# Row 1's sums of the first norm on ScalarE, and four operation orders written anew

## The chip, the core and the metric

The kernel runs on one core of one Trainium2 chip. The metric is the time of one execution on the device in microseconds (us); times are medians over runs. The engines are PE (TensorE: PE for matmuls, PEld for weight loads), DVE (VectorE), ACT (ScalarE), POOL (GpSimd) and SP (SyncE, which here only issues DMAs). ACT and POOL issue DMAs too.

## The reference

Two pairs of layers on x, 2048 rows of 512 bf16 values:

```python
x = x + _A_ref(_layernorm(x), A_w_r, A_w_i)
x = x + _B_ref(_layernorm(x), B_w1, B_w2, B_w3, B_w4)
x = x + _A_ref(_layernorm(x), A_w_r, A_w_i)
x = x + _B_ref(_layernorm(x), B_w1, B_w2, B_w3, B_w4)
```

`_A_ref` is a two-dimensional real FFT over rows and columns, a product with complex weights, and the inverse FFT. `_B_ref` is an MLP mixer: norm, times w1 (512 by 512), gelu, a shift of the four quarters of the columns by -1, +1, -2, +2 rows, times w2, a residual sum; then norm, times w3 (512 by 1792), gelu, times w4, a residual sum.

## The kernel before

The 2048 rows lie as 128 partitions times 16 slots q ("rows" 0 to 15 below are these slots: 128 x 512 each). The FFT is done as matmuls with tables (T, FL, TL, TR, G, Tinv). The program is `first_front` (the norm and first transform of the input), then `layer` twice, called layer A (`last` false) and layer B (`last` true) here. A layer is one FFT mixing and one MLP mixing; layer A ends with the norm and first transform that layer B starts from.

No scheduler orders the work. Each stage is a small function with a letter, and the strings `ORDER_0`, `ORDER_A`, `ORDER_B` list them by hand-readable tokens: letter, number, for some the engine (A ScalarE, V VectorE, P GpSimd, D VectorE from PSUM), and after a dot the first PSUM bank. Each engine takes its own operations in the order of the string, and so does the DMA queue of SP; an operation that has to wait holds up all behind it on its engine.

Tokens of `ORDER_0`: `s` sums of a row (bn_stats on VectorE, L278, or for the rows in `ON_ACT` a mean and a square on ScalarE, L353 and L290), `i` their aggregation (L306), `f` the variance from ScalarE's sums of a group (three GpSimd operations, L359 to L361; after that of group 2 the first tables are loaded), `S` the square root on ScalarE (L365) and `J` the reciprocal on VectorE (L368) for a group of `GROUPS`, `Q` the scaled table Tq of a row (L384, L386), `O` the matmuls of a pair of rows (L403), `G` and `L` the copies from PSUM to V (two halves for the last ones). Behind them GpSimd issues the loads of `load_rest`: one doubling of W, a small copy that waits for the last Tq (L197), two operations that make half of TL (L238, L239, `turn_TL`), three more doublings (L185), a load of TL and the second load of TR (L184), which the `b` of units above 7 read.

Tokens of a layer, in the order of the data: `d` (L544 to L550), `t`, `q` (L568), `x`, `p` (product with W: L587 for V and P from a copy, L584 for D straight from PSUM), `b` and `V` (L598), `m` and `l`; `D` and `C` (L618), `Y`, `P` (L646), `a` (L654: x plus the transform, with row sums), `s` (L290); `r`, `e`, `i`, `M` the statistics of four rows, `n` the norm of a row (L374, L376), `T` the DMA transpose of two rows on SP (L674); `v` (w1, L686), `h` (gelu), `u` (w2, L702), `f` (L710), `k` (L290), `E` (L717), `R`, `o` (norm), `U` (transpose, L674), `w` (w3, L737), `g` (gelu, L744), `W` (w4, L757), `A` (L763), `y` (store). In layer A the next norm follows: `B` (L278), `j` (L306), `S`, `J`, `Q`, `O` (L413, L403), `G`, `L`, `I`. `N` makes the negative of a part of TR on VectorE (L817), `X` are matmuls on zeros. The `v` and `w` of a group of four rows need both transposes of that group.

Of the kernel before, what the change touches and what calls it, by code (L numbers as in the profile page):

```python
# [11 lines left out]
ACT = mybir.ActivationFunctionType  # L12
ALU = mybir.AluOpType
BF16 = dt.bfloat16
FP32 = dt.float32

P = 128
# [358 lines left out]
            self.K.nc.scalar.activation(dst, src, ACT.Identity, bias=self.mr[:, i, :], scale=r)  # L376


def scaled_T(K, q, r, eng="V"):

    K.Tq[q] = K.stream.tile([P, 2, P], BF16, name="Tq", bufs=8)
    if eng in "VP":
        e = K.nc.vector if eng == "V" else K.nc.gpsimd
        e.tensor_scalar(K.Tq[q][:], K.T[:], r, None, op0=ALU.mult)  # L384
    else:
        K.nc.scalar.activation(K.Tq[q][:], K.T[:], ACT.Copy, bias=0.0, scale=r)  # L386
# [65 lines left out]
def first_front(K):  # L452
# [71 lines left out]
def layer(K, last):  # L524
# [4 lines left out]
    V = K.V  # L529
# [6 lines left out]
    tv, X, pab, Y, xT, xT3, gT, ln, ln3, lnA = [{} for _ in range(10)]  # L536
# [251 lines left out]

    def scale_T(n, eng):
        k, i = divmod(n, 4) if n < 12 else (n, 0)  # L790
        scaled_T(K, ROWS[n], lnA[k].r[:, i:i + 1], eng)

    def front(k):
        qs = [ROWS[n] for n in PAIRS[k]]
# [24 lines left out]
    def act_table(k):  # L819
# [23 lines left out]
WAKE = 30  # L843
FILL = {}
GROUPS = [[0, 1], [2, 3], [4, 5, 6, 7], [8, 9, 10, 11], [12, 13], [14, 15]]
ON_ACT = [5, 9]
TABLES = 2
FIRST = [[0, 1], [2, 3], [4, 5], [6, 7], [8, 9], [10, 11], [12, 13], [14], [15]]
UNITS = {b: [b, b + 1] if 2 <= b < 14 else [b] for b in (0, 1, 2, 4, 6, 8, 10, 12, 14, 15)}
# [7 lines left out]
ROWS = [*range(2, 16), 0, 1]  # L857
PAIRS = {**{k: [2 * k, 2 * k + 1] for k in range(7)}, 14: [14], 15: [15]}
PLAIN = 6
FLEX = "mlGLnotxYIKEpQ"  # L860
FOLD = [(), ()]
ORDER_0 = """
s1 s0 i1 i0 S0 s2 s5 J0 Q0A Q1A s4 s7 s6 i4 f2 O0.4 i7 i6 S2 s3 J2 i2 s9 Q6V Q7V O3.0 i3 s11 S1 J1 s10 Q4A Q2A Q5A G3A
s8 i11 i10 i8 s12 f3 O2.2 Q3P O1.6 S3 J3 Q11P s13 i12 Q10A O5.0 s15 G0A i13 Q8A Q9P S4 G2A s14 i15 J4 Q12V i14 O4.4 S5
J5 Q15V G1A G5V Q13P O6.2 L5A O8.0 Q14V O7.6 G4A G6V G7A L7A G8V L6V L8V
"""
ORDER_A = """
d2.2 t2V d0.6 t0A d1.0 d4.4 N0 q0.6 t1A q2.2 d6.0 x0V p0V q1.6 t4A q4.4 x2A d10.2 t6A d8.0 p1D b1.6 p2P t10A b0.7
q10.2 p4D m0V t8A q6.0 d14.4 m1A d12.6 x10A t14V p10V x6A d15.2 t12A p6V b2.5 b4.3 m4A q14.0 q12.6 x14A q8.3 p12D b3.0
m2A b10.1 b11.5 x8A b7.4 t15A p14P q15.2 b5.6 b14.7 m10A b6.1 m11A b12.5 m7A m5A m3A b13.4 m6A p8V b8.6 m12A p15D b9.0  # L870
m8A b15.2 m15A V12.1 m13V V13.3 l12A m14V V15.4 V14.5 m9V l15V D3.0 l14V D1.6 l13A C1 C3 D0.2 C0 Y1A P3.4 P2.5 Y0A Y3V
a3 s3 P6.0 a2 s2 P1.1 P0.6 a1 a0 s1 P7.2 D2.4 C2 D5.6 s0 a7 s7 D7.2 C5 Y2V P5.1 r0 e0 i0 a6 Y5A a5 D4.4 s6 s5 P4.0 M0
n3V a4 n0V n2P s4 n1P D6.6 C7 C6 Y6A P11.0 T1 C4 P10.1 Y7V P15.2 r1 e1 a11 P12.3 i1 M1 n7V T0 Y4A n6V s11 n5A T3 P13.6
P9.5 n4V a10 s10 P8.4 a8 s8 v1.0 a9 s9 P14.7 a13 s13 h1 v0.4 a14 T2 c0 h0 r2 n8P v3.6 h3 v2.0 h2 n9V T4 a15 c1 n10V
n11V u0.5 a12 u3.4 u1.0 f3 u2.1 s12 f2 s14 s15 r3 n14V T5 v5.2 n15V v4.6 c3 T7 k3 h5 u4.1 n12V h4 u7.4 n13V f0 k0 T6
u6.5 f1 k1 u5.6 c2 E3V f7 E7V E2V f4 k2 R0 o2V f6 o3A v6.2 h6 v7.0 h7 f5 E1P E6V o1P k4 E0V o0V u12.4 k6 k7 k5 R1 U1
o7A u9.5 u15.3 f9 U0 u13.1 f12 E12V u10.7 k12 E4P u14.0 u11.5 o6P U3 E5V o5A f15 u8.2 w0.3 k15 E9P g0 f8 k8 o4P f11
E11V k11 w4.5 g4 w3.2 f14 k14 f10 w2.4 E10P g3 E8P w5.2 w1.6 g2 E14V g5 U2 w7.2 g1 f13 k13 R3 w6.0 k9 k10 w8.5 g6 W3.7
A3 B3 g8 W2.0 R2 A2 B2 o9P o10A W1.5 W0.0 g7 A1 B1 o11A U5 o8A j1 E15V U4 w14.2 g14 w11.4 w12.2 g11 w9.4 w10.6 g9 j2
w13.4 E13P g12 g10 g13 W7.1 o13V W5.2 A0 w17.4 W4.0 j3 B0 w16.6 j0 S0 Q2V Q3V A7 A4 Q1P B7 o12P W6.3 A5 A6 B6 g16 j7  # L880
w15.0 g15 w19.2 g19 B4 w18.0 g18 g17 w20.6 j4 j6 g20 o14A B5 W11.0 j5 S1 U6 Q6V W9.1 Q4P o15P U7 A11 B11 w21.6 Q5A
O2.2 O1.4 Q7A G1A j11 A9 B9 W8.0 G2A G2V Q0P O0.2 G1V A8 I1V I2V B8 j8 g21 w24.6 W10.1 A10 B10 j10 G0A g24 w23.6 j9 S2
Q11P Q9P g23 w22.0 O3.4 w26.6 g22 w27.0 G3A G3V G0V g26 Q8P I3V w25.4 g27 I0V g25 W13.2 A13 B13 j13 O4.0 G4A G4V I4V
W12.3 A12 B12 j12 S12 S13 J13 Q13P J12 W15.1 A15 B15 j15 S15 J15 Q15A W14.2 W24.5 Q12A Q10V O5.6 A14 A24 O6.2 G5A B14
B24 j14 S14 G6A J14 Q14A L6A O15.0 G15A L15A O14.2 G14A G5V I5V L14A
"""
# [17 lines left out]


# [28 lines left out]
```

## Time and profile before

| what | value |
|---|---|
| median of 3 runs | 345.87 us (345.47 to 346.12) |
| the profiled execution | 346.01 us, its span 344.2 us |
| granted TensorE clock, mean | 1.000 |
| first matmul of the first transform (L403) | 7.73 us |
| first matmul of layer A's products (L544) | 19.36 us, the next ones from 19.77 |
| first L618 of layer A | 37.06 us |
| first matmul of w1 in layer A (L686) | 51.76 us |
| first matmuls of layer B's products | 183.64 us |
| first matmul of w1 in layer B | 216.47 us |
| last operation of VectorE (L763) | 341.29 us, 0.29 us long |

Busy time in stretches, in us of each engine:

| stretch | PE | DVE | ACT | POOL |
|---|---|---|---|---|
| 0 to 10 | 7.59 | 5.65 | 4.96 | 3.54 |
| 10 to 20 | 9.68 | 8.69 | 8.96 | 7.93 |
| 20 to 30 | 10.00 | 9.07 | 8.96 | 7.19 |
| 30 to 40 | 10.00 | 8.53 | 8.59 | 1.92 |
| 185 to 200 | 14.47 | 13.98 | 14.93 | 5.50 |

Times in the profile count from the start of the span. Matmuls overlap in the records, so a busy PE can still hide small waits; the starts of the matmuls tell them. A few matmul records are missing, which shows as a gap of one pitch more.

### The profile page before, as it was taken

How to read it: one execution, taken by the hardware profiler on the slowest of the kernel's cores; microseconds unless marked ns; L12 is line 12 of the kernel's file. 1: busy time of each engine (PE TensorE's matmuls, PEld its weight loads, DVE VectorE, ACT ScalarE, POOL GpSimd, SP SyncE). 2: the span in 40 equal slices, each digit the busy share in tenths (PEclk: the TensorE clock that was granted, in tenths of full speed). 3: DMA queues.
4: the chain of work that ended last, by engine and by line, in shares of the span. 5: the costliest groups of instructions: out<-in, count | busy, mean ns of one | idle time of the engine just before them, and what ended most of it. 6: DMA issues, size and time to landing. Idle time of an engine off the chain costs nothing.

```text
span 344.2 us, 5699 instructions
## 1 busy us (share of the span) xinstructions
PE 335.5 (97%) x2171; PEld 187.6 (55%) x2189; DVE 165.0 (48%) x377; ACT 195.6 (57%) x357; POOL 107.1 (31%) x200
## 2 busy tenths in 40 slices
PE   7999999999999999999999999999999999999996
PEld 5878974444444444454467888444444444444443
DVE  4889895685035015264676979647802000110122
ACT  4979899768752403534538979968681446014300
POOL 2884066668242000304011404765591000000000
PEclk9999999999999999999999999999999999999999
DMA  7986986333030100300000002541403500000121
GB/s 257 314 295 230 372 202 113 72 61 62 3 61 0 32 0 0 31 2 0 2 0 2 2 3 47 104 81 20 89 0 76 109 0 0 30 18 5 41 78 46
DMA packets 45259, 24.60 MB, mean 71 GB/s; under 512 B 35072, under 2 KB 42240, under 8 KB 45232
## 3 DMA queue, kind: packets, MB, share of 16 engines
q1 hardware_dynamic: 43760, 19.74, 23.5%
q0 software_dynamic: 1232, 4.40, 3.7%
q8 instruction: 17, 0.28, 0.3%
q10 hardware_dynamic: 240, 0.10, 0.1%
q14 instruction: 10, 0.08, 0.1%
HBM read 11.61 MB, written 2.10 MB: 40 GB/s over the span
## 4 chain that ended last, share of the span: by engine, by line
PE 87%; DMA 4%; DVE 4%; ACT 2%; issue 1%; SPq 0%; POOL 0%; ACTq 0%; DVEq 0%; POOLq 0%
PE ps L737 28%; PE ps L757 26%; PE ps L686 8%; PE ps L702 8%; PE ps L598 4%; PE ps L403 3%; PE ps L618 3%; PE ps L568 2%; DMA xT<-xn 2%; PE ps L550 2%; PE ps L646 2%; DMA x_state<-in_A_x_dram 1%; DVE x_state L654 1%; ACT xn L290 1%; ACT gT L744 1%
## 5 line engine op out<-in xcount | busy, mean ns | idle before, releaser
L744 ACT ACTIVATE gT<-ps 128x1024 bf16<-128x1024 f32 x56 | 55.8, 1022 | 86.1 <-PE ps L737 86.1
L737 PE MATMUL ps<-xT,w 128*128 128x512 bf16 x448 | 99.2, 379 | 0.5 <-DMA xT<-xn 0.5
L757 PE MATMUL ps<-w,gT 128*128 128x512 bf16 (+2 forms) x462 | 97.8, 366 | 0.7
L763 DVE TENSOR_TENSOR x_state<-ps,x_state 128x512 bf16<-128x512 f32 (+2 forms) x34 | 22.2, 659 | 124.5 <-PE ps L757 124.5
L757 PEld LDWEIGHTS <-gT 128*128 128x128 bf16 x476 | 45.5, 98 | 51.4
L737 PEld LDWEIGHTS <-w 128*128 128x128 bf16 x448 | 43.7, 98 | 53.1 <-DMA xT<-xn 1.0
L710 DVE SCALAR_TENSOR_TENSOR xn<-xn,ln_c,ps 128x512 bf16<-128x512 bf16 x32 | 23.0, 743 | 15.5 <-PE ps L702 8.8
L686 PE MATMUL ps<-xT,w 128*128 128x512 bf16 x128 | 28.9, 379 | 0.7 <-DMA xT<-xn 0.4
L702 PE MATMUL ps<-w,hT 128*128 128x512 bf16 x124 | 28.3, 379 | 0.2
L290 ACT ACTIVATE junk<-xn 128x512 bf16<-128x512 bf16 x32 | 19.7, 622 | 4.8 <-DVE xn L710 4.8
L278 DVE BATCH_NORM_STATS2 ln_st<-x_state 128x6 f32<-128x512 bf16 (+2 forms) x31 | 20.2, 663 | 3.9 <-DMA x_state<-in_A_x_dram 3.6
L654 DVE SCALAR_TENSOR_TENSOR x_state<-ps,x_state 128x512 bf16<-128x512 f32 x32 | 20.7, 684 | 1.3 <-PE ps L646 1.2
L686 PEld LDWEIGHTS <-w 128*128 128x128 bf16 x128 | 12.3, 98 | 15.9 <-issue 1.7
L702 PEld LDWEIGHTS <-hT 128*128 128x128 bf16 x128 | 12.4, 98 | 15.3 <-ACT hT L693 0.4
L290 ACT ACTIVATE xn<-x_state 128x512 bf16<-128x512 bf16 x32 | 19.8, 620 | 0.9 <-DVE x_state L654 0.7
L693 ACT ACTIVATE hT<-ps 128x512 bf16<-128x512 f32 x32 | 17.4, 601 | 4.6 <-PE ps L686 4.4
L313 POOL TENSOR_SCALAR ln_ve<-ln_mv 128x4 f32<-128x4 f32 x11 | 2.8, 257 | 54.6 <-DVE ln_mv L306 53.9
L646 PE MATMUL ps<-Y,Tinv 128*128 128x256 bf16 x128 | 16.0, 272 | 0.1
L598 PE MATMUL ps<-TR,PB 128*128 128x128 bf16 x256 | 16.0, 219 | 0.0
L584 DVE TENSOR_TENSOR PB<-ps,W 128x1024 bf16<-128x1024 f32 x13 | 15.4, 1217 | 0.7 <-PE ps L568 0.5
L618 PE MATMUL ps<-G,hT 128*128 128x256 bf16 x128 | 15.7, 272 | 0.0
L403 PE MATMUL ps<-Tq,x_state 128*128 128x256 bf16 (+1 forms) x160 | 14.0, 246 | 1.6 <-ACT Tq L386 1.0
(95 smaller groups left out, 405.9 us busy)
## 6 DMA issues: line engine op xcount, KB each, us to landing
w<-in_B_w_dram SPq DMA_DIRECT2D x2, 1792.0 KB, 14.3
W<-W POOLq DMA_DIRECT2D x4, 514.0 KB, 5.0
x_state<-in_A_x_dram SPq DMA_DIRECT2D x8, 256.0 KB, 4.7
out_dram<-x_state SPq DMA_DIRECT2D x15, 128.0 KB, 1.9
w<-in_B_w_dram SPq DMA_DIRECT2D x2, 512.0 KB, 6.2
W<-in_A_w_r_dram SPq DMA_DIRECT2D x7, 128.5 KB, 5.8
W<-in_A_w_i_dram SPq DMA_DIRECT2D x7, 128.5 KB, 5.9
TL<-tab_TL POOLq DMA_DIRECT2D x3, 256.0 KB, 5.4
```

The costliest lines, as they stand in the source:

```text
L290: K.nc.scalar.activation(out, src, ACT.Square, bias=0.0, scale=D ** -0.5, accum_out=self.s[:, i, 1:2])
L403: K.nc.tensor.matmul(dst, lhsT=K.x[:, q, c * P:(c + 1) * P], rhs=rhs, start=(j == 0), stop=(j == 3))
L598: nc.tensor.matmul(o[:, k0 * P:(k0 + 1) * P], lhsT=pab[u][:, k, 2 * (b - u) + h, f * P:(f + 1) * P], rhs=K.TR[:, k:k + 2, 2 * b + h], star ...
L618: nc.tensor.matmul(o[:, i, e * 256:(e + 1) * 256], lhsT=M[:, F, e, 2 * m + i, :], rhs=K.G[:, F, e, :], start=(F == 0 and e == 0), stop=(F ...
L646: nc.tensor.matmul(o[:, h * 256:(h + 1) * 256], lhsT=K.Tinv[:, c], rhs=rhs[:, ::-1] if h else rhs, start=(e == 0), stop=(e == 1))
L654: nc.vector.scalar_tensor_tensor(K.x[:, q, :], ps.pop(("P", q)), 1.0, K.x[:, q, :], op0=ALU.mult, op1=ALU.add, accum_out=ln[g].s[:, i, 0:1])
L686: nc.tensor.matmul(o[:, i], lhsT=K.w1[:, t, j * P:(j + 1) * P], rhs=xT[g][:, :, t, :], start=(t == 0), stop=(t == 3))
L702: nc.tensor.matmul(o, lhsT=K.hT[:, j, st:st + P], rhs=K.w2[:, j, :], start=(j == 0), stop=(j == 3))
L710: nc.vector.scalar_tensor_tensor(xn[:, q, :], xn[:, q, :], ln[q // 4].c[:, q % 4:q % 4 + 1], ps.pop(("u", n)), op0=ALU.mult, op1=ALU.add, ...
L737: nc.tensor.matmul(o[:, i], lhsT=K.w3[:, c, t * P:(t + 1) * P], rhs=xT3[g][:, :, c, :], start=(c == 0), stop=(c == 3))
L744: nc.scalar.activation(gT[g][:, 2 * j:2 * j + 2, :], ps.pop(("w", k)), ACT.Gelu_apprx_tanh, bias=0.0, scale=1.0)
L757: nc.tensor.matmul(o, lhsT=gT[g][:, t, i * P:(i + 1) * P], rhs=K.w4[:, t, d], start=(t == 0), stop=(t == 13))
```

## The change

Row 1 joins `ON_ACT`, so that its sums are made by ScalarE instead of VectorE. `scaled_T` can make one half of the table alone (`signs=1`), and does so for the rows whose transform needs no more (rows n below 12 in layer A). All three orders are replaced; in them many operations change their engine and their place. The orders were made with a rule that an operation of VectorE and one of GpSimd that both work on SBUF exclude each other in time.

```diff
-def scaled_T(K, q, r, eng="V"):
+def scaled_T(K, q, r, eng="V", signs=2):
...
-    K.Tq[q] = K.stream.tile([P, 2, P], BF16, name="Tq", bufs=8)
+    K.Tq[q] = K.stream.tile([P, signs, P], BF16, name="Tq", bufs=8, padded_shape=[P, 2, P])
...
-        e.tensor_scalar(K.Tq[q][:], K.T[:], r, None, op0=ALU.mult)
+        e.tensor_scalar(K.Tq[q][:], K.T[:, 0:signs], r, None, op0=ALU.mult)
...
-        K.nc.scalar.activation(K.Tq[q][:], K.T[:], ACT.Copy, bias=0.0, scale=r)
+        K.nc.scalar.activation(K.Tq[q][:], K.T[:, 0:signs], ACT.Copy, bias=0.0, scale=r)
...
-        scaled_T(K, ROWS[n], lnA[k].r[:, i:i + 1], eng)
+        scaled_T(K, ROWS[n], lnA[k].r[:, i:i + 1], eng, 1 if n < 2 * PLAIN else 2)
...
-ON_ACT = [5, 9]
+ON_ACT = [1, 5, 9]
...
 ORDER_0 = """
-s1 s0 i1 i0 S0 s2 s5 J0 Q0A Q1A s4 s7 s6 i4 f2 O0.4 i7 i6 S2 s3 J2 i2 s9 Q6V Q7V O3.0 i3 s11 S1 J1 s10 Q4A Q2A Q5A G3A
-s8 i11 i10 i8 s12 f3 O2.2 Q3P O1.6 S3 J3 Q11P s13 i12 Q10A O5.0 s15 G0A i13 Q8A Q9P S4 G2A s14 i15 J4 Q12V i14 O4.4 S5
-J5 Q15V G1A G5V Q13P O6.2 L5A O8.0 Q14V O7.6 G4A G6V G7A L7A G8V L6V L8V
+s0 s1 i0 s5 s2 s3 s4 i3 i2 f0 S0 S1 i4 J0 Q0A Q1A s7 J1 Q3A O0.5 Q2A O1.0 s6 i7 i6 f2 S2 s9 f3 s10 J2 i10 Q5A Q4V O2.2
+s11 s8 Q6V G0A i11 i8 S3 s13 Q7A J3 Q8A G1A i13 O3.4 s12 i12 S4 s14 Q9P O4.6 s15 i14 Q10A G3A i15 S5 J4 Q12V J5 Q11P
+Q13V O5.0 G2A L5V O6.4 Q14P O7.2 G4A G7A G5V Q15V L7A O8.0 G8A G6V L6V L8A
 ORDER_A = """
-d2.2 t2V d0.6 t0A d1.0 d4.4 N0 q0.6 t1A q2.2 d6.0 x0V p0V q1.6 t4A q4.4 x2A d10.2 t6A d8.0 p1D b1.6 p2P t10A b0.7
...
-m2A b10.1 b11.5 x8A b7.4 t15A p14P q15.2 b5.6 b14.7 m10A b6.1 m11A b12.5 m7A m5A m3A b13.4 m6A p8V b8.6 m12A p15D b9.0
...
-P9.5 n4V a10 s10 P8.4 a8 s8 v1.0 a9 s9 P14.7 a13 s13 h1 v0.4 a14 T2 c0 h0 r2 n8P v3.6 h3 v2.0 h2 n9V T4 a15 c1 n10V
...
-w15.0 g15 w19.2 g19 B4 w18.0 g18 g17 w20.6 j4 j6 g20 o14A B5 W11.0 j5 S1 U6 Q6V W9.1 Q4P o15P U7 A11 B11 w21.6 Q5A
...
-W12.3 A12 B12 j12 S12 S13 J13 Q13P J12 W15.1 A15 B15 j15 S15 J15 Q15A W14.2 W24.5 Q12A Q10V O5.6 A14 A24 O6.2 G5A B14
-B24 j14 S14 G6A J14 Q14A L6A O15.0 G15A L15A O14.2 G14A G5V I5V L14A
+d2.3 d0.6 d1.2 N0 t2V d4.0 t0A q0.6 t1V q2.4 d6.2 t4A x2A q1.0 p0D t6A d10.6 t10A q4.4 d8.2 t8A p1D d12.0 q10.6 p4D
...
+p6V p12D b11.5 b10.1 b7.0 x8A m10A q15.6 m5A x15A b6.2 p8V b12.1 m12A b3.4 m6V p15V m11A b9.3 b13.1 b8.2 b14.5 m7V m3A
...
+a5 s5 C4 n1P r1 T0 D7.2 n2V P10.1 n3V C7 P11.0 Y4V Y7A D6.6 C6 P9.2 e1 P8.4 i1 M1 P15.3 a11 a9 Y6A n4P P13.7 T1 n5A
+P12.0 T2 a10 a8 a13 s11 n6P s9 s8 n7P s10 P14.5 r2 a14 n9V v1.1 h1 v0.5 a15 T3 h0 s13 v3.1 c0 n11V s15 h3 v2.4 n10V T5
...
+o10A g2 w11.0 g11 w7.2 g7 g5 w10.0 w12.2 g12 W1.7 A1 B1 j1 o8A U4 E12V w13.4 g13 o12P U7 W0.6 A0 B0 W2.2 w9.5 g9 W3.3
+o11P U5 E13V o13A U6 A2 B2 A3 j0 B3 j2 j3 S0 Q0V Q3V w8.4 w20.6 g10 Q1V g8 w14.0 w19.2 g20 w15.4 g14 W5.0 A5 W7.6 g19
...
+W14.0 G4V I4P A12 B12 j12 S12 J12 A13 W24.4 Q12A B13 J15 Q15A Q10V j13 S13 J13 A14 A24 B14 O5.2 B24 j14 G5A O15.6 G15A
+L15V Q13P O6.0 S14 J14 Q14A O14.4 G6A L6A G5V G14A L14A I0P I5V
 ORDER_B = """
-X3.4 d4.1 d15.0 t15V d12.5 d1.7 t4A q4.0 t1V t12A q15.2 d0.4 d2.6 p15D x4A q1.0 d8.2 t0A q0.4 t2A t8A q2.6 p1D x0A
-q12.0 x12A d10.2 q8.4 p2D d14.0 p4P b4.1 d6.6 p12V m4V t10A x8A b3.2 b5.5 q10.3 t6A t14A q6.6 m5A b12.0 m3A b2.1 m12A
-b1.5 p8V b8.0 p0P b9.2 x6A b0.6 b15.7 m8A p10D q14.3 m1A p6V m9A p14D b11.0 m2A b10.2 m0A b6.1 b7.6 b14.3 m11A m10V
...
+X6.6 d15.2 d1.1 d4.4 t15A q15.6 p15D d12.2 t1A d0.0 t4A q4.4 t0V t12A q1.6 x4A p1D d2.1 t2A d14.0 t14A d8.4 q0.6 x0A
+q12.2 x12A q2.0 p4V b5.6 m5A b15.7 m15A t8V q8.4 x8A d10.6 t10A d6.2 p0P b1.4 p2D t6A b4.1 b0.0 m0A p8V q10.6 p12V
+q6.2 b2.0 m1A m4A x6A b8.4 p10D b3.1 b12.5 b9.3 b13.2 p6V q14.6 m2A b11.0 m12A m11V b10.5 m3A m8A x14A b7.1 p14V m9A
...
+P15.2 n1P a11 s11 P14.7 T2 a8 v2.3 a10 a15 s8 T1 s10 c0 r2 T0 v3.5 a12 s15 v1.1 n11P n10V s12 h2 T5 c1 a13 h1 v0.3 h3
...
```

No instruction is added beside the three operations of GpSimd and the two of ScalarE for row 1's sums (in place of VectorE's), and three matmuls on zeros; the rest moves between engines and places.

## The prediction

> **What bounds the kernel now.** I read the page first, its busy shares and slices, then the table of stretches, then TensorE's waits, then the chain that ended last.
>
> ```profile
> PE 335.5 (97%) x2171; PEld 187.6 (55%) x2189; DVE 165.0 (48%) x377; ACT 195.6 (57%) x357; POOL 107.1 (31%) x200
> ...
> PE   7999999999999999999999999999999999999996
> PEld 5878974444444444454467888444444444444443
> DVE  4889895685035015264676979647802000110122
> ACT  4979899768752403534538979968681446014300
> ```
>
> TensorE is busy 97% of the span; VectorE and ScalarE come near full in two places, slices 2 to 6 and 22 to 25 (8.6 us each): the first norm with the Fourier products of layer A, and the Fourier products of layer B. Everywhere else they idle beside TensorE. No matmul is added or taken but three fillers (X3.4 becomes X6.6, 3 x 0.11 us, in a wait). So the change is worth what it does to TensorE's waits, and I counted these from the starts of the matmuls (each start minus the start before, less the usual pitch): 0.07 us from 60 to 85, nothing from 85 to 140 and from 240 to the end, 1.4 from 140 to 185, 3.1 from 185 to 200, about 1 each in 40 to 60 and 200 to 240. TensorE begins real work at 7.73. The new orders can gain or lose only there, and a new wait in a quiet stretch counts in full.
>
> ```profile
> PE ps L403 <- ACT Tq L386: 1.0, 2, 0.8
> ...
> PE ps L403 <- DVE Tq L384: 0.6, 1, 0.6
> PE ps L568 <- DVE PB L584: 0.5, 1, 0.5
> PE ps L737 <- DMA xT<-xn: 0.5, 1, 0.5
> PE ps L686 <- DMA xT<-xn: 0.4, 1, 0.4
> ```
>
> These are the longest waits: in us, how often, the longest. Each is a place to follow in the new orders. I did so by hand: every engine takes its operations in the written order, each with the duration of its row before.
>
> **The first norm (the named part).** Before, row 1 is a bn_stats on VectorE (0.66). After, it is two activations on ScalarE (L353, L290), 1.23 a row as row 5 shows (5.96 to 7.19), and three small GpSimd operations (L359 to L361), ending about 0.75 after the sums (f2: 7.19 to 7.95). Rows 0 and 1 land at 4.2, so row 1's sums run 4.22 to 5.45, row 5's (landed 5.9) 5.92 to 7.15; S0 was at 5.76 and now stands behind them: 7.15 to 7.44. S1 goes in front of Q0A, J0 behind s2, s3, s4, i3, i2, i4 on VectorE: J0 7.54, Q0A 7.74 to 8.23. First matmul 8.28 against 7.73: **0.55 later**. But Q3A (8.53) and Q2A (8.93 to 9.42) follow at once, so O1 starts with no wait at O0's end, 9.6; before, TensorE stood still until here:
>
> ```profile
> 9.78 9.12 PE ps L403 x108
> 18.92 0.72 ACT V L154 x2
> ```
>
> From there I find each Tq ready in time (0.1 lost at row 7), O8 ends at 18.8, L6V and L8A end at 19.35, and layer A's products start at 19.45 instead of 19.77: **-0.3**.
>
> **What hangs on the last Tq.** GpSimd's loads wait for it (gate, L197): Q14V ends at 17.57 before, Q15V at 18.05 after. Then come turn_TL (1.63 and 0.75), three W doublings, TL2 and the second TR load, which is just in time now:
>
> ```profile
> TR<-tab_TR POOLq DMA_DIRECT2D x1, 768.0 KB, 7.9
> ```
>
> Issued at 23.26, landed 31.1; its first user, b10, starts at 31.21. GpSimd waits 0.72 before the last doubling, which takes up part of a delay; from below nothing, from above 0.5 plus a 0.5 meeting with N0: it lands at 31.1 to 32.1. The products themselves, followed unit by unit, bring b11 to 31.45 (gaps at d10, q14 and b5) and the next stage, D1, to 37.05, where D3 starts at 37.06 before: the 0.3 is gone there. With TR 0 to 0.6 late I take **+0.2** at this point (bounds 0 and 0.6).
>
> N0, a VectorE operation from SBUF to SBUF, now stands before t2V and meets turn_TL; in the trace it runs at 21.71, after turn_TL's end at 20.2, so no row shows that meeting. The Trainium skill ("SBUF — State Buffer", section "Who interferes with whom") says that GpSimd and such an operation hold a shared port in turn and the second waits for the whole instruction. By it N0 waits until 19.98, the loads move 0.5 more, and the forecast would be 345.4. A nearer row for a meeting is n3V beside n1P at 46.08: 0.83 instead of 0.41, 0.42 lost; the loads' bound above is that row, rounded up.
>
> **The first MLP's entry.** All sixteen P now stand before v1; before, P14 stood after it while v1 waited 0.56 at 51.76 for T0. T1 lands at 51.75 after (n2V, n3V end at 47.75, two transposes of 1.26 and 3.3 to landing). h1 no longer stands behind s13, v3 waits for T3 (55.4) about 0.1. The first u comes at 59.0 instead of 59.27: **-0.3** (bounds -0.5 and 0).
>
> **The last transpose of layer A.**
>
> ```profile
> 138.79 2.86 ACT gT L744 x3
> 141.65 0.70 ACT xn L376
> ...
> 142.42 4.57 DMA xT<-xn
> ...
> 147.03 1.90 PE ps L737 x8
> ```
>
> Row 15's norm (o14A) stood behind three gelus, its transpose landed at 147.0, and w21 waited: the start gap there is 0.67 over pitch. After, U7 is written before W0 and U6 after B0, some 20 us ahead of w27, their first user: **-0.65**. Unless another wait takes its place (nothing I followed does), all of it is gained.
>
> **From layer A to B.** After the last W4, A24, B24, j14, S14 stay; L15V (0.42) is put before J14, and G6A and L6A behind Q14A, where G15A and L15A stood (0.5 each against 0.27). L14A ends at 183.65 against 183.86, but I5V ends at 183.75 against 183.50. d15 starts around 183.5 to 183.8 against 183.64: **-0.1** (bounds -0.3 and +0.3).
>
> **Layer B's products.** Here the exclusion is to be seen:
>
> ```profile
> 192.13 2.20 DVE L587 TENSOR_TENSOR PB<-X,W 128x2048 bf16<-128x2048 bf16 x1
> ...
> 194.85 1.21 DVE L587 TENSOR_TENSOR PB<-X,W 128x2048 bf16<-128x2048 bf16 x1
> ```
>
> ```profile
> 187.74 5.50 POOL L587 TENSOR_TENSOR PB<-X,W 128x2048 bf16<-128x2048 bf16 x2 [10.54 <-ACT X L154]
> ```
>
> The same VectorE product takes 2.20 while GpSimd's p0P runs (to 193.24) and 1.21 alone: 0.98 lost, in a chain of VectorE operations without a gap (p2D, p12V, m4V, p8V, p10D) at whose end TensorE waits 0.69 at 198.38. After, p4 goes from GpSimd to VectorE (1.22), t8 too (1.22 against 0.69 for t15), p14 reads SBUF (0.69 against 1.21), and copies go to ScalarE and back; p0P runs beside t8V and p2D, which read PSUM. VectorE's sum is 17.4 against 17.1 with the 0.98 in it; ScalarE's grows by 0.2. So the loss is not simply gained: it is spent on p4. Following the units I get D3 at 201.3 against the first D at 202.17, **-0.9**; by the sums alone it is +0.15. I take half, -0.45, as I cannot rule out small gaps of 0.1 on a chain of 30 operations.
>
> **Layer B's MLP entry.** v2 waits for its transpose at 216.47; followed through a4 to a7, r1, e1, i1, n7P, n6P, T3, T2, it starts at 216.4: 0 (bounds -0.3, +0.3). The first w3 (244.5 before, U1 landed 244.03) has U1 at 243.5 and w6 at 244.1 after: no wait. Norms on GpSimd go from 3 to 5 in A and 3 to 6 in B; each meeting with VectorE costs 0.42 by the row above, off the path where I followed it. Rows 0, 1 and the last W4s, the A20 and its store are as before: tail 0.
>
> **Sum.** Front to D1 +0.2, MLP entry -0.3, w21 -0.65, hinge -0.1, B's products -0.45: -1.3. Waits that I did not find can only add; I put 0.2 for them: **-1.1**. Against the profiled execution's own 346.01 (span 344.2 and 1.8 around it) this is **344.9**; the median before is 345.87, 0.14 lower, so about -0.3%. A change under 0.2% (0.7 us) cannot be told from none.
>
> **Rivals.**
> 1. *The walk holds in full* (nothing lost to small gaps, B's products -0.9, TR in time): 0 - 0.3 - 0.65 - 0.1 - 0.9 = -1.95, 344.1. For it: TensorE's slack everywhere else; against: both vector engines 90% full there. Chance 0.17.
> 2. *No change*: B's products +0.15 because VectorE's sum did not shrink, TR 0.6 late, the rest as forecast: 0.6 - 0.3 - 0.65 - 0.1 + 0.15 + 0.2 = -0.1, 345.9. Chance 0.26.
> 3. *The first norm comes late and takes the loads along* (slower). S0 waits for ScalarE's four sums, S1 stands before Q0A, J0 behind four bn_stats: every Tq depends on one in-order chain. If the last Tq comes 2 us later than my 18.05, d2 starts 1.7 after 19.77, turn_TL, the doublings and TR come 2 late, and b11 waits as long: +2.2 in place of +0.2 gives 346.9. From about 1.1 us late it outweighs the gains, from 1.65 the result is slower by over 0.2%. For it: J0 and S0 move by over 1.2 us; against: rows 2 to 5 are summed by then, and TensorE has O0's 1.3 us to cover. Chance 0.22.
> The forecast itself: 0.35. That the exclusion is already absent in other places or not the planner's doing changes nothing here; the written orders are what runs.
>
> So faster 0.17 + 0.35 = 0.52, within 0.2% 0.26, slower 0.22. The range runs from rival 1 with the MLP entry at its bound of -0.5 (343.9) to rival 3's 346.9.
>
> **What would show it.** First matmul of L403 near 8.3 and hardly a gap after it; first L544 near 19.4; no wait at the first b over 7 (L598 near 31.4); no 0.5 us wait for a transpose in L737; no VectorE L587 over 1.3 us; the first L618 of layer B under 18 us after its first L544. I am wrong if a wait appears between 85 and 140 or after 240, where there is none now, or if L598 waits for TR.

## The result, and the profile after

Six runs of the changed kernel have a median of 343.89 us (343.40 to 344.89), six of the kernel before 346.32 (345.47 to 347.24). The ratio is 0.9945, with a 95% interval of 0.993 to 0.996: about 1.9 us faster by the ratio (1.4 to 2.4 by its interval; the two medians lie 2.4 apart). The profiled execution took 344.65 us with a span of 342.9, against the forecast 344.9, and the granted clock was 0.999. Another set of runs of the same program, with its own runs of the kernel before (345.87), gave 344.52 and 0.9957 (0.994 to 0.9974); its profile has a span of 341.9. The page of the changed kernel:

```profile
PE 334.4 (98%) x2175; PEld 187.0 (55%) x2192; DVE 163.2 (48%) x370; ACT 195.8 (57%) x360; POOL 108.2 (32%) x210
...
PE   6999998999999999999999999999999999999996
...
DVE  5889794577005212544387989665812000010122
ACT  6979899687651521522438989978771343146000
```

The busy shares hardly moved: VectorE has 1.8 us less, GpSimd 1.1 more. They tell nothing of the gain. TensorE's waits do:

```profile
PE ps L403 <- DMA x_state<-in_A_x_dram: 1.8, 1, 1.8
PE ps L686 <- DMA xT<-xn: 1.0, 1, 1.0
PE ps L262 <- DVE zeros L253: 1.0, 1, 1.0
PE ps L598 <- DMA TR<-tab_TR: 0.4, 1, 0.4
```

The waits for Tq inside the first transform, for PB at L568 and for xT at L737 are gone. In their place stand one wait ahead of the first transform, one of 1.0 at the first w1 (L686) of layer A, and 0.4 for TR. (The one on the zeros comes before any real work.) The start gaps over pitch, summed by stretch, say where it matters (the sums depend a little on which pitch is taken as the usual one): 0.7 to 0.8 us less than before from 185 to 200 and 0.8 to 1.0 less from 140 to 185, but 0.6 to 0.8 more from 20 to 40 and some 0.4 more from 40 to 60; nothing from 60 to 140 and from 240 on, so no new wait in the quiet stretches.

The following table sets the predicted terms beside the profiles. A term is the difference to before in the time between two checkpoints (first matmuls of a line; D1 is the first L618 of A):

| stretch | predicted | after | the same program again |
|---|---|---|---|
| start to D1 (before 37.06) | +0.2 | +0.10 | -0.04 |
| D1 to the first w2, L702, of A (22.05) | -0.3 | +0.35 | -0.56 |
| from there to layer B's first L544 (124.53) | -0.75 | -0.99 | -0.99 |
| layer B's products, to its first L618 (18.37) | -0.45 | -0.50 | -0.50 |
| from there to its first L686 (14.47) | 0 | -0.20 | -0.20 |
| from there to the last matmul (124.56) | 0 | -0.12 | -0.06 |
| not found | +0.2 | | |
| sum | -1.1 | -1.35 | -2.33 |

Only the second line differs much between the two profiles of the same program. That is the wait of 1.0 at L686.

### The profile page after: what moved, and what is told of

Read it like the earlier page. It is cut to its first block, busy times and chain, and to the rows that moved or that the text cites. A ratio compares the mean times of both kernels' runs of the same rounds, so it can differ in the third digit from the quotient of the medians.

```text
span 342.9 us, 5718 instructions
## 1 busy us (share of the span) xinstructions
PE 334.4 (98%) x2175; PEld 187.0 (55%) x2192; DVE 163.2 (48%) x370; ACT 195.8 (57%) x360; POOL 108.2 (32%) x210
## 4 chain that ended last, share of the span: by engine, by line
PE 86%; DMA 8%; ACT 2%; SPq 2%; DVE 1%; issue 1%; POOL 0%; POOLq 0%; DVEq 0%
PE ps L737 28%; PE ps L757 28%; PE ps L686 8%; PE ps L702 8%; PE ps L598 4%; DMA W<-in_A_w_i_dram 3%; PE ps L618 3%; DMA TR<-tab_TR 2%; PE ps L646 2%; PE ps L568 1%; ACT xn L290 1%; PE ps L550 1%; DMA T<-tab_T 1%; DMA xT<-xn 1%; SPq L231 1%
## 5 line engine op out<-in xcount | busy, mean ns | idle before, releaser
L737 PE MATMUL ps<-xT,w 128*128 128x512 bf16 x448 | 99.0, 379 | 0.0
L737 PEld LDWEIGHTS <-w 128*128 128x128 bf16 x448 | 43.8, 98 | 52.9
L686 PE MATMUL ps<-xT,w 128*128 128x512 bf16 x128 | 28.7, 379 | 1.0 <-DMA xT<-xn 1.0
L702 PE MATMUL ps<-w,hT 128*128 128x512 bf16 x124 | 28.2, 379 | 0.2
L686 PEld LDWEIGHTS <-w 128*128 128x128 bf16 x128 | 12.3, 98 | 16.2 <-issue 1.7
L278 DVE BATCH_NORM_STATS2 ln_st<-x_state 128x6 f32<-128x512 bf16 (+2 forms) x30 | 19.4, 663 | 3.7 <-DMA x_state<-in_A_x_dram 3.3
L702 PEld LDWEIGHTS <-hT 128*128 128x128 bf16 x128 | 12.4, 98 | 15.2 <-ACT hT L693 0.5
L598 PE MATMUL ps<-TR,PB 128*128 128x128 bf16 x256 | 16.0, 219 | 0.4 <-DMA TR<-tab_TR 0.4
L618 PE MATMUL ps<-G,hT 128*128 128x256 bf16 x128 | 15.9, 272 | 0.0
L598 PEld LDWEIGHTS <-PB 128*128 128x128 bf16 x256 | 14.5, 98 | 2.2 <-issue 2.0
```

The lines of the kernel that those rows point to most:

```text
L598: nc.tensor.matmul(o[:, k0 * P:(k0 + 1) * P], lhsT=pab[u][:, k, 2 * (b - u) + h, f * P:(f + 1) * P], rhs=K.TR[:, k:k + 2, 2 * b + h], star ...
L618: nc.tensor.matmul(o[:, i, e * 256:(e + 1) * 256], lhsT=M[:, F, e, 2 * m + i, :], rhs=K.G[:, F, e, :], start=(F == 0 and e == 0), stop=(F ...
L686: nc.tensor.matmul(o[:, i], lhsT=K.w1[:, t, j * P:(j + 1) * P], rhs=xT[g][:, :, t, :], start=(t == 0), stop=(t == 3))
L702: nc.tensor.matmul(o, lhsT=K.hT[:, j, st:st + P], rhs=K.w2[:, j, :], start=(j == 0), stop=(j == 3))
L737: nc.tensor.matmul(o[:, i], lhsT=K.w3[:, c, t * P:(t + 1) * P], rhs=xT3[g][:, :, c, :], start=(c == 0), stop=(c == 3))
```

## The experiments

Two theories were to be told apart. Mine: the gain is made of one-place repairs (a transpose asked for earlier, a VectorE product kept clear of a GpSimd one), and the part that the change is named for carries nothing. The rival: the front carries the gain, through everything that hangs on the last Tq. All ratios are to the kernel before, run on the same chip, with 95% intervals. In the diffs, three dots stand for lines left out, and of some lines of an order only the tokens that matter are shown.

**The three parts, each alone.** The kernel before with the new front, row 1 on ScalarE and the new `ORDER_0`:

```diff
-ON_ACT = [5, 9]
+ON_ACT = [1, 5, 9]
...
 ORDER_0 = """
-s1 s0 i1 i0 S0 s2 s5 J0 Q0A Q1A s4 s7 s6 i4 f2 O0.4 i7 i6 S2 s3 J2 i2 s9 Q6V Q7V O3.0 i3 s11 S1 J1 s10 Q4A Q2A Q5A G3A
...
+s0 s1 i0 s5 s2 s3 s4 i3 i2 f0 S0 S1 i4 J0 Q0A Q1A s7 J1 Q3A O0.5 Q2A O1.0 s6 i7 i6 f2 S2 s9 f3 s10 J2 i10 Q5A Q4V O2.2
...
```

> The kernel before with the new ORDER_0 and row 1 in ON_ACT alone; layers A and B keep their old orders. Theory (the front's gain is taken back by the second TR load, which waits for the last Tq and for the loads of W): the first L544 comes 0.5 to 0.6 us earlier than 19.36, the first b above 7 waits for TR (31.7 against 31.21), the first L618 is at 37.1 to 37.6 as before or later, and the time is unchanged to 0.5 us longer (ratio 1.000 to 1.0015). Rival (the named part carries the gain): the 0.5 to 0.6 us reach the first L618 and the end, ratio 0.998.

Measured: 0.9994 (0.998 to 1.0007). The path of the theory is not in this profile: rows 4 and 5 landed late, the first L544 came at 19.59 and not half a microsecond earlier, and no wait for TR is in the list. The first L618 is at 37.22, as expected.

The kernel before with layer A's new order and the half tables:

```diff
-def scaled_T(K, q, r, eng="V"):
+def scaled_T(K, q, r, eng="V", signs=2):
...
 ORDER_A = """
-d2.2 t2V d0.6 t0A d1.0 d4.4 N0 q0.6 t1A q2.2 d6.0 x0V p0V q1.6 t4A q4.4 x2A d10.2 t6A d8.0 p1D b1.6 p2P t10A b0.7
...
+d2.3 d0.6 d1.2 N0 t2V d4.0 t0A q0.6 t1V q2.4 d6.2 t4A x2A q1.0 p0D t6A d10.6 t10A q4.4 d8.2 t8A p1D d12.0 q10.6 p4D
...
```

> The kernel before with the new ORDER_A and the halved Tq alone. Theory (parts add up, and A's gain is the wait of w21 and the hinge to layer B, less a later first u): first u up to 0.4 us later than 59.10, no wait in L737, the first L544 of layer B 0.4 to 0.9 us earlier than 183.64, ratio 0.9975 to 0.999. The transpose T0 took 2.16 us to issue in the profile after, against 1.23 to 1.33 for all others: if that is due to the order it is 2.1 to 2.2 here again, and v1 waits over 1 us; if it was chance, it is 1.3 and v1 starts near 51.8. Rival (the gain comes with the front or layer B): ratio 1.000 or above.

Measured: 0.9968 (0.9956 to 0.998), a larger gain than expected. L737 has no wait, and from the first w2 to layer B it takes 123.80 us against 124.53. In the profile this is lost again, as the first w2 is 0.8 late and the first L544 of layer B at 183.69: T0 took 2.33 us, which the expectation would have read as the order's doing; but the next kernel, with layer A's old order, has 2.14, so the order is not the cause.

The kernel before with layer B's new order:

```diff
 ORDER_B = """
-X3.4 d4.1 d15.0 t15V d12.5 d1.7 t4A q4.0 t1V t12A q15.2 d0.4 d2.6 p15D x4A q1.0 d8.2 t0A q0.4 t2A t8A q2.6 p1D x0A
...
+X6.6 d15.2 d1.1 d4.4 t15A q15.6 p15D d12.2 t1A d0.0 t4A q4.4 t0V t12A q1.6 x4A p1D d2.1 t2A d14.0 t14A d8.4 q0.6 x0A
...
```

> The kernel before with the new ORDER_B alone. Theory (the product that stood still beside GpSimd's is freed, and the entry of the MLP is a little earlier): L587 on VectorE nowhere over 1.3 us, from the first L544 of layer B to its first L618 17.8 to 18.0 us instead of 18.36, end 0.7 to 0.9 us earlier, ratio 0.9975 to 0.998. Rival (what was taken from the exclusion was put back on VectorE as p4, nothing gained): 18.3 to 18.5 us, ratio 0.9995 to 1.0005.

Measured: 0.9977 (0.996 to 0.9993), as expected; layer B's products took 17.72 us, and no L587 of VectorE in them took over 1.3 (one in layer A's products, at 28.4, took 1.61). The three gains, 0.0006, 0.0032 and 0.0023, add to 0.006, and the whole change has 0.0055: within their intervals the parts add. The named one shows no gain of its own; its interval allows at most 0.002.

**Why the front earns nothing.** In the changed kernel ScalarE and TensorE begin so:

```profile
5.63 0.63 ACT L353 ACTIVATE junk<-x_state 128x512 bf16<-128x512 bf16 x1
...
6.88 0.54 ACT L365 ACTIVATE ln_r<-ln_mv,eps 128x2 f32<-128x2 f32 x2
7.39 1.71 ACT L386 ACTIVATE Tq<-T,ln_r 128x256 bf16<-128x256 bf16 x4
```

```profile
7.95 1.26 PE L403 MATMUL ps<-Tq,x_state 128*128 128x256 bf16 x13 [1.76 <-DMA x_state<-in_A_x_dram]
```

The columns are start, duration, engine, line, operation; the bracket is the idle time before it and what ended it. Row 5's sums start the moment rows 4 and 5 have landed (5.61), and the square roots S0 and S1, which need only rows 0 to 3, stand behind them in the written order; the first Tq and the first matmul follow, 2.34 us after that landing. So the new order ties the first matmul to the third load of x. In the front alone that load landed at 6.38, and the first matmul came at 8.72, again 2.34 later; the five profiles with this order have 2.33 or 2.34. In the order of before, where S0 stands ahead of row 5, it comes 1.81 to 2.2 after the same landing (5.90 and 7.73 in the profile of before). What the front loses there it gets back by starting O1 at once: layer A's first L544 is at 18.8 to 19.6 in the profiles with the new front and at 19.0 to 19.4 in those with the old one.

Row 1 alone, taken back to VectorE in the changed kernel:

```diff
-ON_ACT = [1, 5, 9]
+ON_ACT = [5, 9]
...
-s0 s1 i0 s5 s2 s3 s4 i3 i2 f0 S0 S1 i4 J0 Q0A Q1A s7 J1
+s0 s1 i0 i1 s5 s2 s3 s4 i3 i2 S0 S1 i4 J0 Q0A Q1A s7 J1
```

> The kernel after with row 1's sums back on VectorE (bn_stats and its aggregation, no GpSimd operations for group 0), all orders otherwise as after. Theory (the end of layer A's products is set by TR, so the front has slack): the first matmul of L403 moves by less than 0.5 us, the first L618 of layer A by less than 0.2, and the time is that of after, ratio to before 0.994 to 0.9955. Rival (ScalarE's sums for row 1 are what made the front 0.6 us shorter, and it counts): first L544 0.5 us or more later than 18.82 and the time 0.5 us above after's.

Measured: 0.9965 (0.9951 to 0.998), not to be separated from the change itself (0.9945, 0.993 to 0.996, and 0.9957, 0.994 to 0.9974). Its first matmul came 0.7 us later (2.86 after the third load of x instead of 2.34), its first L544 at 19.54, and its first L618 at 37.55, 0.4 to 0.5 later than in the two profiles of the change, where less than 0.2 was expected:

```profile
PE ps L403 <- DMA x_state<-in_A_x_dram: 2.9, 1, 2.9
```

So within the new order row 1 on ScalarE does bring the first transform forward, by some 0.5 us. In the one profile this lasts to the first L618; what of it reaches the end cannot be told from nothing in these times. The old front under the new layers says the same from the other side; here `ORDER_0` is that of before, and the rest the changed kernel:

```diff
-ON_ACT = [1, 5, 9]
+ON_ACT = [5, 9]
...
-s0 s1 i0 s5 s2 s3 s4 i3 i2 f0 S0 S1 i4 J0 Q0A Q1A s7 J1 Q3A O0.5 Q2A O1.0 s6 i7 i6 f2 S2 s9 f3 s10 J2 i10 Q5A Q4V O2.2
...
+s1 s0 i1 i0 S0 s2 s5 J0 Q0A Q1A s4 s7 s6 i4 f2 O0.4 i7 i6 S2 s3 J2 i2 s9 Q6V Q7V O3.0 i3 s11 S1 J1 s10 Q4A Q2A Q5A G3A
...
```

> The kernel after with the old ORDER_0 and row 1's sums on VectorE: the named part undone with its order. Theory (the front's gain hangs on when rows 4 and 5 land, and what is left of it is waited away before the first L618): first L618 37.0 to 37.4, the rest as after, ratio 0.9945 to 0.996, no more than 0.3 us from after_again. Rival (row 1 on ScalarE is worth its 0.5 us): 0.5 us or more above after_again.

Measured: 0.995 (0.9933 to 0.9967), 344.21 us; the first L618 is at 37.56, a little later than expected. No loss without the new front can be seen.

**One transpose.** In the kernel before, one token moved, the norm of row 15 in layer A:

```diff
-g20 o14A B5
+g20 B5
...
-o8A j1 E15V
+o8A o14A j1 E15V
```

> The kernel before with one token moved: o14A (row 15's norm on ScalarE) from behind g20 to behind o8A, so that its transpose U7 is issued right behind U6, some 25 us earlier. Theory (the wait of w21 is removed and nothing takes its place): no wait of L737 for a transpose, the first L544 of layer B 0.65 to 0.7 us earlier after the first u (123.9 against 124.54), ratio 0.998. Rival (the next late thing, W11 or the Q of rows 8 to 11, takes the wait over): 124.3 to 124.6 us, ratio 1.000.

Measured: 0.998 (0.9969 to 0.999). From the first w2 of A to layer B's first L544 it takes 123.86 us against 124.53: 0.67 less, which is the whole gap at w21 in the profile of before. The wait for xT at L737 is gone from its list. That this one token earns is shown; by the ratios it is about a third of the change's gain (0.002, interval 0.001 to 0.0031, of 0.0055). The gap is not the same in every execution: with o14A at its old place it is 0.34, 0.36, 0.66 and 0.77 in the profiles of four other kernels.

**The meeting in layer B's products.** In the kernel before, p0 from GpSimd to VectorE, so that p12V meets no GpSimd product:

```diff
-b1.5 p8V b8.0 p0P b9.2 x6A
+b1.5 p8V b8.0 p0V b9.2 x6A
```

> The kernel before with p0 of layer B on VectorE instead of GpSimd (p0P becomes p0V), so that p12V no longer runs beside a GpSimd product. Theory (exclusion): p12V takes 1.21 us instead of 2.20, p0V adds 0.69, the wait of q14 falls from 0.69 to about 0.4, from the first L544 of layer B to its first L618 18.05 instead of 18.36, ratio 0.999. Rival (p12V is long for another reason, its inputs or PSUM): p12V stays at 2.2, the stage takes 18.7 to 19.1, ratio 1.001 to 1.002.

Measured: 0.9985 (0.9972 to 0.9998). VectorE's product p12V takes

```profile
191.96 1.22 DVE L587 TENSOR_TENSOR PB<-X,W 128x2048 bf16<-128x2048 bf16 x1
```

where it took 2.20, and the stage 17.99 us against 18.37, though VectorE has p0 to do as well. The other three profiles in which p12V meets p0P have 2.20 to 2.22 again. That shows the exclusion: work taken from GpSimd and given to the engine that was full made the stage end earlier. Before, a full block until p0P's end (193.24) gives 193.24 + 1.21 = 194.45 for p12V's end, and it ended at 194.33. The Trainium skill ("SBUF — State Buffer", section "Who interferes with whom") has GpSimd and a VectorE operation with two SBUF inputs contend, which agrees with this pair.

The other move of the change, p4 to VectorE, alone:

```diff
-p2D d14.0 p4P b4.1
+p2D d14.0 p4V b4.1
```

> The kernel before with p4 of layer B on VectorE instead of GpSimd (p4P becomes p4V), the main move of the new order for the products. GpSimd's p0 then runs two us earlier, away from p12V. Theory (the 0.98 us gained from the exclusion is spent on p4's 1.22): p12V 1.21 us, from the first L544 of layer B to its first L618 18.4 to 18.7, ratio 1.000 to 1.001. Rival (the move alone makes the gain of layer B): 17.9 to 18.1, ratio 0.9985 or less.

Measured: 1.0031 (1.0015 to 1.0048), slower, and in the profile the stage takes 20.96 us, 2.6 more than before, where a few tenths were expected. Its TensorE, its VectorE, and then the table of stretches (length, busy time and instructions of PE, PEld, DVE, ACT and POOL, then the granted clock, the DMA share and GB/s):

```profile
193.39 0.62 PE L598 MATMUL ps<-TR,PB 128*128 128x128 bf16 x8 [1.69 <-DVE PB L587]
```

```profile
191.85 2.63 DVE L587 TENSOR_TENSOR PB<-X,W 128x2048 bf16<-128x2048 bf16 x2
...
197.75 2.36 DVE L584 TENSOR_TENSOR PB<-ps,W 128x1024 bf16<-128x1024 f32 x2 [1.53 <-PE ps L568]
```

```profile
192.00:193.00 1.00, 0.00 (x0) 0.00 (x0) 1.00 (x1) 0.80 (x2) 0.25 (x1) 1.00 0.00 0
...
194.00:195.00 1.00, 1.00 (x9) 0.78 (x7) 1.00 (x2) 0.00 (x0) 0.00 (x0) 0.50 0.00 0
195.00:196.00 1.00, 1.00 (x11) 0.95 (x9) 1.00 (x2) 0.71 (x1) 0.00 (x0) 0.50 0.00 0
...
198.00:199.00 1.00, 1.00 (x21) 0.93 (x18) 1.00 (x2) 0.58 (x3) 0.00 (x0) 1.00 0.00 0
```

Three costs follow one another. p4V stands behind p1D and p2D on VectorE and begins at 191.85; it now is the one that meets p0P (until 192.25) and takes 1.49 of the 2.63, p12V only 1.22. b4, which reads it, stands where it stood, right behind, in TensorE's queue, and holds up all that follows for 1.69 us. Then the granted clock falls to 0.50 for some 3.4 us (0.96 in the row from 193 and 0.83 in the one from 197, which are not shown): 9 to 11 matmuls fit in a microsecond instead of 21. And the d and q behind b4 come late, so that VectorE in turn waits 1.53 for q10. The clock explains why this profiled execution (348.58) lies 1.6 above the median of its kernel (346.98): 3.4 us at half speed cost at most 1.7. The mean granted clock is known for every run: three of the twelve have 0.995 and are above 348.5, the other nine have 0.999 or 1.000 and lie between 346.5 and 347.6. So the fall comes in some executions only. Without it the stage would take some 19.3 us by the same estimate, still more than expected.

In the changed kernel p4 is on VectorE too, at 188.17, ahead of t8 and p2D, and b4 comes after d10, d6 and three other b:

```profile
188.17 1.22 DVE L587 TENSOR_TENSOR PB<-X,W 128x2048 bf16<-128x2048 bf16 x1
...
192.70 2.36 DVE L587 TENSOR_TENSOR PB<-X,W 128x2048 bf16<-128x2048 bf16 x2
```

```profile
189.93 1.92 POOL L587 TENSOR_TENSOR PB<-X,W 128x1024 bf16<-128x1024 bf16 x1 [8.67 <-ACT X L154]
```

The second fence is GpSimd's p0P, from 189.93 to 191.85: VectorE has t8V and products from PSUM (L584) beside it, and no L587. That is the exclusion obeyed. VectorE's busy time in the stage stays as it was, 15.83 us against 15.86, while GpSimd's falls from 5.50 to 1.92, and the stage is 0.5 us shorter. That p4 on VectorE does no harm here because b4 has a later place is argued from the two orders; no run moves b4 alone.

**The second TR load.** It is the last load of the front, and b11 waits 0.4 us for it. In the changed kernel, issued one step earlier:

```diff
         double(2)
-        double(3)
         load_TR(1)
+        double(3)
```

> The kernel after with the second TR load issued before the last doubling of W, so that it does not stand behind the doubling's wait for the loads of W. Theory (the second TR load is what takes the front's gain back): TR lands about 1 us earlier (30.5 to 30.9), L598 waits no more for it, the first L618 of layer A comes 0.3 to 0.5 us earlier than 37.16 (when the first L544 is at 18.8), unless p12D then waits for the doubling; ratio to before 0.9935. Rival (the two vector engines set the end of that stage): the first L618 stays within 0.15 us, the time is after's.

Measured: 1.0036 (1.0011 to 1.0062), slower; what the theory had named as its exception happened. TensorE's waits, and then GpSimd:

```profile
PE ps L598 <- DVE PB L584: 1.1, 1, 1.1
...
PE ps L544 <- DVE PB L584: 1.0, 1, 1.0
```

```profile
32.99 1.92 POOL L587 TENSOR_TENSOR PB<-X,W 128x1024 bf16<-128x1024 bf16 x1 [4.86 <-DMA W<-W]
```

TR's wait is gone, but TR, issued at 22.3, landed at 31.22; in the two profiles of the unchanged order it was issued at 23.7 and 23.3 and landed at 31.72 and 30.92. So the earlier start brought TR nothing that can be told, and the last doubling of W landed at 32.85 against 29.15 and 29.09. The products that read that W come late, on GpSimd as in the row and on VectorE at 32.94, and D1 is at 39.04. The DMA engines have little room there (a share of 0.99 from 10 to 20 us in the profile after, 0.85 from 20 to 40), so it looks as if the order of the loads only chose which is late. Part of the loss in the times is the clock: four of the twelve runs have a granted clock of 0.995 and take 348.3 to 350.3, the other eight 345.1 to 347.1.

**Chance and what is left.** Once more the changed kernel, without any edit:

> The kernel after, unchanged, beside the next three on the same chip. Theory (the first transpose of layer A is slow in some executions, whatever the order): ratio to before 0.994 to 0.996; if the first transpose is issued in 1.3 us in this profile, the first u comes near 58.9, else near 59.6.

Measured: 0.9957 (0.994 to 0.9974). T0 took 1.26 us in this profile, there is no wait at L686, and the first u comes at 58.51, 0.4 earlier than the expected 58.9. Next, the old front once more, and layer A's products too in the order of before, up to its `l15V`, with the new order of A from D1 on:

```diff
-d2.3 d0.6 d1.2 N0 t2V d4.0 t0A q0.6 t1V q2.4 d6.2 t4A x2A q1.0 p0D t6A d10.6 t10A q4.4 d8.2 t8A p1D d12.0 q10.6 p4D
...
-D1.2 D3.4 l13A l14A C1 C3
+d2.2 t2V d0.6 t0A d1.0 d4.4 N0 q0.6 t1A q2.2 d6.0 x0V p0V q1.6 t4A q4.4 x2A d10.2 t6A d8.0 p1D b1.6 p2P t10A b0.7
...
+l14V l13A D1.2 D3.4 C1 C3
```

> The kernel after with the old ORDER_0 and, in layer A, the old order of the products up to the first D; from there all as after. Theory (the new order of layer A's products is 0.3 to 0.6 us longer from its first L544 to its first L618, 18.0 to 18.3 against 17.65, all other parts of after are gains): first L618 36.8 to 37.1, ratio 0.9935 to 0.9945, 0.2 to 0.4 us below after_again. Rival (both orders end when the loads of TR and W let them): as old_front.

Measured: 0.9943 (0.993 to 0.9957). From the first L544 to D1 it takes 17.70 us, as before, where the new order takes 18.0 to 18.6 (and 20.1 with TR's load first); D1 is the earliest of all at 36.73. In the runs the 0.3 cannot be told apart from the change. And both halves of every table made again:

```diff
-        scaled_T(K, ROWS[n], lnA[k].r[:, i:i + 1], eng, 1 if n < 2 * PLAIN else 2)
+        scaled_T(K, ROWS[n], lnA[k].r[:, i:i + 1], eng, 2)
```

> The kernel after with the full Tq (both signs) made for all rows in layer A. Theory (the Tq of rows below 12 are early, nothing waits for them): ratio as after_again within 0.1%. Rival (GpSimd's longer Tq, 0.92 instead of 0.60 to 0.67, and the longer meetings delay the last rows): first L544 of layer B 0.2 us or more later after the first u than 123.54.

Measured: 0.9951 (0.9933 to 0.997), 344.26 us, and the first L544 of layer B 123.54 after the first u: the half tables are worth nothing that can be measured. No kernel of these beats the changed one beyond the intervals.

## Why the prediction came out right, point by point

**The first matmul**: forecast 8.28, measured 7.95. The step rested on rows 4 and 5 landing at 5.9; they landed at 5.61, and the delay from there, 2.34, is nearly the 2.38 of the working. The landing lies between 5.61 and 6.38 in the five profiles with the new `ORDER_0`, and all of that shows in the first matmul.

**The first norm, -0.3 at layer A's products**: the products came earlier than forecast, the first L544 at 18.82 and the next matmul at 19.15 (19.36 and 19.77 before; the forecast 19.45 was for the second of these), but they did not hold it. As forecast, the gain is gone at D1 (+0.10 and -0.04; forecast +0.2). In the first profile L598 waits for TR:

```profile
23.66 8.06 DMA TR<-tab_TR
31.76 1.50 PE ps L598 x24
```

This is the chain that ended last: the wait ends with the landing at 31.72 (31.13 before), inside the bounds of 31.1 to 32.1. I had listed "L598 waits for TR" as something that would make me wrong; it happened, and cost no more than the term had room for. But TR is not the whole of it. In the second profile it landed at 30.92 and nothing waits for it, and from the first L544 to D1 it still takes 18.01 us, as in the two other profiles of the new order without a listed wait there; with the wait it is 18.34, before it was 17.70. Five of the seven profiles with the old order have 17.64 to 17.70. So some 0.3 us goes to the new order of the products, and TR's wait took another 0.3 in the first. The working had the 0.3 gone by small gaps in the products; which of them it is no run takes apart.

**N0 beside turn_TL**: the row against the rule. Here VectorE's N0 does run during GpSimd's L238:

```profile
17.88 1.82 POOL L238 TENSOR_SCALAR TL<-TL 128x512 bf16<-128x512 bf16 x1
```

```profile
18.66 0.41 DVE L817 TENSOR_SCALAR TR<-TR 128x1024 bf16<-128x1024 bf16 x1
```

N0 took 0.41, no more than alone (0.42 to 0.50 in the profiles where it comes later), and L238 1.82 in place of 1.63: 0.19 lost, by the operation that was first, in all five profiles with this pair. The rule that the prediction weighed (the Trainium skill, "SBUF — State Buffer", section "Who interferes with whom"), by which N0 would have stood until L238's end, is contradicted here, and with it the 345.4 that it gave. But in the two profiles where N0 met L239, the copy behind L238, N0 took 0.90 and 0.94 and the copy its usual 0.75. So the rule fits one pair of operations and not the other. Why is open.

**The first MLP's entry, -0.3**: right in kind, hidden by chance in the profile shown.

```profile
49.27 3.25 DMA xT<-xn
52.66 3.40 PE ps L686 x15
```

The chain waits for the second transpose, T1, which SP could issue only at 49.27: the first, T0, took 2.17 us to issue (47.01 to 49.17). In the second profile of the same program T0 took 1.26, T1 was issued at 48.22, and the first w1 starts with no wait:

```profile
48.70 2.79 PE L646 MATMUL ps<-Y,Tinv 128*128 128x256 bf16 x24
51.51 2.75 PE L686 MATMUL ps<-xT,w 128*128 128x512 bf16 x12
```

The five profiles of the new layer-A entry with the usual T0 have 21.49 to 21.98 from D1 to the first w2, against 22.05: -0.1 to -0.6, and -0.3 was the term. The slow T0 also stands in profiles with layer A's old order (1.87 and 2.14 us), so the new order is not its cause. It costs this execution some 0.9 us (22.40 against 21.49), about what it lies above its median. That the forecast 344.9 came so near to its 344.65 is therefore luck: the sum was 1.1, the profile without the slow T0 is 2.3 us shorter than the one before, and the two sets of medians are 2.4 and 1.35 us faster.

**w21, -0.65, and the hinge, -0.1**: measured -0.99 together, the same to 0.01 us in the seven profiles with both new layers. The transpose is 0.67 of it (the single token shows it). Of the rest I took a third: layer A's order alone gives 123.80, and with the start of layer B's order it is another 0.26 less. The wait for xT at L737 is in no list of a kernel with the new order of A.

**Layer B's products, -0.45**: -0.50 measured, half of what the full walk gave (-0.9). Halving it was a guess about small gaps, and that the size came out right is luck: the eight profiles with the new order of B have 17.72 to 18.23 us, which is -0.65 to -0.14. That p4's move costs some 1 us by itself, with b4 at its old place, was in no step. **Layer B's entry**: 0 forecast, -0.20 measured, inside its bounds. **The 0.2 for waits not found** was not needed: nothing new appeared after 60 us.

So what was mis-sized was small terms that add up: hinge and entry of B 0.4 too small, the reserve 0.2 too large, and the MLP's entry between. Rival 3 (the front late, the loads along with it) fell: the last Tq's gate left L238 starting at 17.88 against 17.89. Rival 2 fell in layer B's products: its premise held, VectorE's busy time did not shrink (15.86 and 15.83 us), yet the stage is 0.5 us shorter and not 0.15 longer, so the sum of VectorE's work does not set its length. Rival 1's time, 344.1, is the nearest to the medians, though not its reason: it had -0.9 from layer B's products and little at the hinge.

## What to carry to other kernels

Where TensorE is busy 97% of the span, list its start gaps stretch by stretch first: an order of hundreds of tokens was worth what it did to some four gaps, and one token gave about a third of it. Moving one operation to another in-order engine is not priced by its duration but by who reads it and what stands behind that reader: p4 on VectorE alone costs about 1 us, and in the new order, where b4 comes later, the stage is 0.5 shorter. And look whether a gain in the named place lasts: 0.5 us at the start of a stage was worth nothing here, where the stage's end hung on a load and on its own small gaps.

## What was not expected of the hardware

A gap of 1.69 us in TensorE's work was followed by some 3.4 us at a granted clock of 0.50 (p4 on VectorE alone); one of 2.87 ahead of the first matmul (row 1 taken back) was not, nor were gaps of 1.0 and 1.1 us in the profile with TR's load first. By the clocks of the single runs such a fall comes in 3 of 12 runs with p4 on VectorE, 4 of 12 with TR's load first, 1 of 12 with row 1 taken back and 1 of 8 of the changed kernel run again (0.994 or 0.995 each), and in none of the kernel before. The Trainium skill ("TensorE: Matmul & The Clock Gate", section "HAM oscillation — how this bites in real kernels") warns of gaps over about 3.4 us; this one was half as long, so the length of the gap alone does not decide it. What does, the runs do not show; nor do they show that the gap was the cause.

The first DMA transpose took 1.87 to 2.33 us to issue on SP in five of fourteen profiles, where the other nine had 1.26 to 1.28 and the 31 transposes behind it 1.23 to 1.63; and the first w1 of layer A waits for it (from D1 to the first w2 these five took 22.26 to 22.93 us, 0.4 to 1.1 more than their like). In all five a packet of 16 KB of the instruction queue q8, at about 45 us, took 2.6 to 3.8 us, and T0's issue ended 0.49 us after that packet in each of them. In eight of the other nine the packet took 1.05 to 1.16 us and was done about 1 us or more before T0's issue ended; in the ninth it took 3.2 but was done 0.53 before, just in time. So the slow T0 goes with a late packet of instructions; why the packet is slow in some executions is open.

The pair N0 and L238 ran together at a price of 0.19 us, while N0 and the copy L239 excluded each other at about 0.5. And a load of 768 KB issued 1.0 to 1.4 us earlier landed no earlier than can be told from the scatter (31.22 against 30.92 and 31.72), at the cost of 3.7 us for the one that it overtook.
